# Who issues the first keys, and when the first weight piece comes: the head of a linear attention and token mixer on one core

## The chip, the cores and the metric

The kernel runs on one core of a Trainium2 chip. The metric is the device time of one execution in microseconds, as the median of several executions. A profiled execution gives the trace.

## The reference

Four batches, four heads, 1088 positions, head size 32. First a linear attention with a quadratic feature map, then a mixer over tokens and channels (all float32 or float64 weights):

```python
def phi(x):                       # S1, S2: 8 x 32
    a = einsum('rd,bhsd->bhsr', S1, x)
    b = einsum('rd,bhsd->bhsr', S2, x)
    return einsum('bhsi,bhsj->bhsij', a, b).reshape(..., 64)
q_p, k_p = phi(q), phi(k)
kv = einsum('bhsf,bhsd->bhfd', k_p, v)
z = sum(k_p, axis=2)
x = einsum('bhsf,bhfd->bhsd', q_p, kv) / (einsum('bhsf,bhf->bhs', q_p, z) + 1e-06)
x = x.transpose(0, 2, 1, 3).reshape(4, 1088, 128)
h = maximum(x.T @ w_tok1, 0) @ w_tok2     # per batch: 1088 -> 256 -> 1088
u = x + h.T
out = u + maximum(u @ w_ch1, 0) @ w_ch2   # 128 -> 1536 -> 128
```

The S matrices and the four weights are float64, so they arrive as pairs of 32-bit words.

## The kernel before

**Tiles and stages.** The sequence is cut into nine tiles of 128 positions (`TILES`) and, for queries and the token mixer, into three chunks of 384, 384 and 320 (`CHUNKS`). For each batch the kernel computes the keys' features and `kv` (`keys`, ops `K<b>.*`), the queries' features `qp` (for batch 0 on TensorE, `queries_on_pe`, ops `Q0.*`; for the others through DRAM, `queries_by_dma`), then attention and token mixing (`mixing`, ops `A<b>.*`), and last the channel mixing (`channel_mix`, ops `U<i>.*`), in which each of 12 slices takes a first group of three matmuls (L992, op `.f`), a Relu on ScalarE (L996, `.h`), a difference on VectorE (L999, `.l`) and a second group of three matmuls (L1005, `.s`). A number is carried as a high and a low half, so one product takes three matmuls. The pool `hid` holds the results of four slices.

**Weights.** `wt1`, `wt2`, `wc1` and `wc2` come in pieces named by two digits, weight and piece: `00` to `04`, `10` to `15`, `20` to `22`, `30` to `32`. `convert` turns a piece of 64-bit floats into 32-bit ones: two ScalarE passes over the words (L363 `.abs`, the magnitude of the high word, and L367 `.low`, the rest of the low word), three VectorE steps (L370 `.clamp`, L374 `.shift`, L377 `.merge`) and an addition on GpSimd (L381 or L383, `.add`). `divide_weight` then makes the halves: ScalarE `.hi` (L474) and VectorE or GpSimd `.lo` (L477). S goes the same way, as the op `s`, and everything of batch 0 needs it: `s_c` is the weight of the keys' matmuls, `s_spread` that of the queries'.

**Order.** The order of the instructions of each engine is made when the kernel is built, by a list scheduler (`Plan.run`): each op has costs by engine, a level (the longest cost behind it, plus a boost for its batch, plus an entry of the table `LEAD`), and of the ops that can start first the one with the highest level goes next. `free` and `dma` in it are the starting times that it assumes for the engines and the transfers. Where it expects TensorE to wait, it puts matmuls on the identity (`fill`, L342).

**Loads.** All loads go out on SyncE's queue (SP) in the order of `LOADS`, each ordered behind the one before it (`load`, L346). The load of S is issued ahead of the plan (L322). In `load_k` the keys of batch 0 are two transfers: columns of the first four tiles (`k0a`, 256 KB) and the rest (320 KB); the first lets `K0.p0` (four tiles) start alone, `K0.p4` takes the other five. The queries of batch 0 are one transfer of 544 KB, and all three `Q0.p<g>` wait for it. A piece of 512 columns is 512 KB, v is 594 KB per batch.

Of the kernel before, what the change touches and what calls it, by code (L numbers as in the profile page):

```python
# [9 lines left out]
F32 = mybir.dt.float32  # L10
# [8 lines left out]
P = 128  # L19
B, H, S, D = 4, 4, 1088, 32  # L20
# [10 lines left out]
TILES = tuple((t * P, P) for t in range(NT))  # L31

CUTS = {0: (2, 2, 2, 2, 1), 2: (4, 4, 4), 3: (4, 4, 4)}
LOADS = "k0 q0 00 v0 01 02 03 04 10 11 20 30 q1 12 13 k1 21 31 v1 14 15 22 32".split()


WIDE = 384
# [2 lines left out]
def _spans():  # L40
# [22 lines left out]
KEYS_ON_POOL = set()  # L63

LEAD = {
    "A0.d2": -161700.0,
    "A0.u0": -740800.0,
    "A0.w2": 67900.0,
    "A1.n2": 62000.0,
    "A1.x": 384700.0,  # L70
    "A1.xT3": 472400.0,
    "A2.w0": -38700.0,
    "A2.w1": -1729700.0,
    "A3.w2": -107200.0,
    "K0.kvz": -142200.0,
    "K0.s08": -237500.0,
    "K1.s": -160000.0,
    "K1.v0": 40800.0,
    "K3.c0": 99700.0,
    "K3.p": 103300.0,  # L80
    "K3.s": -300900.0,
    "K3.v4": -498400.0,
    "Q0.a10": 1269000.0,
    "Q0.a20": 461800.0,
    "Q1.m00": -332100.0,
    "Q1.m10": -30800.0,
    "Q1.p": 115700.0,
    "Q3.p": -1683600.0,
    "U0.f": 988300.0,
    "U0.h": 359200.0,  # L90
    "U0.l": -79900.0,
    "U1.f": 653600.0,
    "U11.f": 345700.0,
    "U2.f": 96300.0,
    "U2.l": -115500.0,
    "U2.s": -804700.0,
    "U4.l": 520500.0,
    "U5.s": -35900.0,
    "U6.s": -144500.0,
    "U8.s": -175400.0,  # L100
    "w00.hi": -357200.0,
    "w00.lo": -624600.0,
    "w00.low": 15500.0,
    "w01.add": -162900.0,
    "w01.hi": -266600.0,
    "w01.lo": -1103500.0,
    "w02.hi": -337700.0,
    "w02.lo": -1981200.0,
    "w03.hi": -871700.0,
    "w03.lo": -604900.0,  # L110
    "w03.low": 376600.0,
    "w03.shift": -580100.0,
    "w04.abs": 1406800.0,
    "w04.add": 140400.0,
    "w04.hi": -260600.0,
    "w04.lo": -663100.0,
    "w04.low": 1049700.0,
    "w10.abs": 830500.0,
    "w10.hi": -265000.0,
    "w10.low": 172800.0,  # L120
    "w10.shift": -115500.0,
    "w11.abs": 656200.0,
    "w11.clamp": -128400.0,
    "w11.low": -9800.0,
    "w12.abs": 1523900.0,
    "w12.clamp": -157100.0,
    "w12.hi": -811900.0,
    "w12.lo": -452800.0,
    "w12.low": 1313100.0,
    "w13.abs": 945800.0,  # L130
    "w13.clamp": -534800.0,
    "w13.hi": 621700.0,
    "w13.low": -19300.0,
    "w13.merge": 637100.0,
    "w13.shift": -290300.0,
    "w14.lo": -1439000.0,
    "w14.low": -519800.0,
    "w15.clamp": 19000.0,
    "w15.low": -641500.0,
    "w21.clamp": 156100.0,  # L140
    "w21.low": -51800.0,
    "w22.abs": 140100.0,
    "w30.clamp": 716200.0,
    "w30.low": -55000.0,
    "w31.hi": -429100.0,
    "w32.low": -49100.0,
}


# [35 lines left out]
class Plan:  # L185
# [20 lines left out]
    def run(self, fill):  # L206
        for op in reversed(self.ops):
            cost = op.weight if op.weight is not None else min(op.ways.values()) + LATE.get(min(op.ways, key=op.ways.get), 0)
            op.level = cost + max((n.level for n in op.next), default=0.0)
        for op in self.ops:  # L210
            op.level += op.boost + LEAD.get(op.name, 0.0)
        free = dict.fromkeys(LATE, 0.0)
        free["sp"], free["act"], free["pe"] = 1060.0, 2000.0, 1400.0 + 427 * WARM
        dma, mode = 2800.0, 0

        port = 0.0
        waiting = {op: len(op.before) for op in self.ops}
        ready = [op for op in self.ops if not op.before]

        def clock(s, cost):  # L220
            if s >= WARMED:
                return s + cost
            return s + 2 * cost if s + 2 * cost <= WARMED else WARMED + cost - (WARMED - s) / 2

        while ready:
            best = []
            for op in ready:
                t = max((a.end for a in op.after), default=0.0)
                ok = True
                for k, h in enumerate(op.takes):  # L230
                    q = self.taken.setdefault(h.pool, [])
                    n = self.bufs.get(h.pool, 1) - sum(o.pool == h.pool for o in op.takes[:k])
                    if len(q) >= n:
                        old = q[len(q) - n]
                        if any(u.end is None for u in old.users):
                            ok = False
                            break
                        t = max(t, max((u.end for u in old.users), default=0.0))
                if not ok:
                    continue  # L240
                for e, cost in op.ways.items():
# [24 lines left out]
            if e == "pool" or (e == "dve" and op.port):
                port = f
            if e == "sp":
                dma = max(dma, f + 630.0) + op.bytes / op.rate
                op.end = dma + (1200 if op.bytes > 100000 else 0)  # L270
            else:
                op.end = f + LATE[e]
            op.emit(e)
            ready.remove(op)
            for n in op.next:
                waiting[n] -= 1
                if not waiting[n]:
                    ready.append(n)
        left = [op.name for op in self.ops if op.end is None]
        assert not left, left[:20]  # L280
# [23 lines left out]
def attn_mixer_kernel(ctx: ExitStack, tc: tile.TileContext, qT, kT, v1, s64, wt1, wt2, wc1, wc2, out):  # L304
# [15 lines left out]

    s_raw = const.tile([P, 64], I64, name="s_raw")
    nc.sync.dma_start(s_raw, s64)  # L322
    ident = const.tile([P, P], F32, name="ident")
    make_identity(nc, ident)
    qp = const.tile([P, 2, SP], F32, name="qp")
# [80 lines left out]
        k_hold[b], q_hold[b], v_hold[b] = Hold("k_sb"), Hold("q_sb"), Hold("v_sb")  # L406
    s_loaded = plan.add("s", {"sp": 0.0}, lambda _: None)
    s_loaded.bytes, s_loaded.rate = 65536.0, 395.0
    prev = s_loaded

    def keep(name, b, shape):
        def dst():
# [3 lines left out]

    def load_k(b, after, boost=0.0):
        if not b:

            half = 4 * P  # L420
            first = load("k0a", lambda: keep("k_sb", 0, [P, SP])()[:, :half], kT[0][:, :half], P * half * 4, after, [k_hold[0]], (), boost)
            k_loaded["first"] = first
            return load("k0", lambda: box["k_sb", 0][:, half:], kT[0][:, half:], P * (SP - half) * 4, [first], (), [k_hold[0]], boost)
        return load(f"k{b}", keep("k_sb", b, [P, SP]), kT[b], P * SP * 4, after, [k_hold[b]], (), boost)

    def load_q(b, after, boost=0.0):
        return load(f"q{b}", keep("q_sb", b, [P, S]), qT[b], P * S * 4, after, [q_hold[b]], (), boost)

    def values(b):
        box["v_sb", b] = new("v_sb", [P, 1200])[:, :NT * H * (D + 1)].rearrange("p (t h d) -> p t h d", t=NT, h=H)  # L430
# [2 lines left out]
    def load_v(b, after, boost=0.0):  # L433
        return load(f"v{b}", lambda: values(b), v1[b], P * NT * H * (D + 1) * 4, after, [v_hold[b]], (), boost)

    k_loaded, q_loaded, v_loaded, doubles = {}, {}, {}, {}
    by_kind = {"q": (load_q, q_loaded), "k": (load_k, k_loaded), "v": (load_v, v_loaded)}
    for name in LOADS:
        if name[0] in by_kind:
            get, known = by_kind[name[0]]  # L440
            b = int(name[1])
            prev = known[b] = get(b, [prev])
# [171 lines left out]
    def queries_on_pe(qp_hold):  # L614
# [16 lines left out]
        for g, (c0, cn) in enumerate(CHUNKS):  # L631
# [12 lines left out]
                            rhs=box["q_sb", 0][rows, cs], start=True, stop=True,  # L644
                        )

            projected = plan.add(f"Q0.p{g}", {"pe": 2 * cn * 1.675 + 20}, project, [q_loaded[0]] + spreads, a_holds + b_holds, [q_hold[0]], 0.0, 2)
            for p in range(2):
                a_hold, b_hold, ar_hold, br_hold = a_holds[p], b_holds[p], Hold("ar"), Hold("ar")

# [461 lines left out]
```

## Time and profile before

| | us |
|---|---|
| three timed runs | 222.3, 221.36, 222.7 |
| median | 222.3 |
| the profiled execution | 223.0 |
| its span, first to last instruction | 220.8 |
| TensorE busy (matmul) | 212.9 |
| VectorE busy | 138.6 |
| ScalarE busy | 118.0 |
| GpSimd busy | 80.3 |

The engines are named PE (TensorE matmul), PEld (its weight loads), DVE (VectorE), ACT (ScalarE), POOL (GpSimd) and SPq or ACTq (the DMA issues of SyncE and of ScalarE). A row of the timeline gives the start, the time, the engine, the line, the operation, the tile written and the tiles read, shapes, a count, and in brackets the engine's idle time before it and what ended that. A row of the waits gives who waited for whom: the total, how often, and the longest. The granted clock of TensorE is 0.998 of full speed.

### The profile page before, as it was taken

The page shows a single profiled execution, that of the slowest core. Times are in us where ns is not written, and L with a number is a line of the kernel's source. Part 1 is how long each engine was busy: PE and PEld are TensorE (multiplying, and loading weights), DVE is VectorE, ACT ScalarE, POOL GpSimd, SP SyncE. Part 2 cuts the span into 40 slices and gives each one's busy share as a digit, 9 for nine tenths or more (in the row PEclk, how much of TensorE's full clock was granted, in tenths as well). Part 3 has the DMA queues.
Part 4 walks back from the last instruction along what each step waited for, and adds up shares of the span by engine and source line. Part 5 has one row for each costly group of instructions (what it writes and reads, how often), then busy time and mean ns, then how long its engine had stood idle before and what let it go on. Part 6 is the DMA issues. An engine that isn't in the chain of part 4 may idle for free.

```text
span 220.8 us, 4921 instructions
## 1 busy us (share of the span) xinstructions
PE 212.9 (96%) x1898; PEld 201.6 (91%) x1898; DVE 138.6 (63%) x273; ACT 118.0 (53%) x284; POOL 80.3 (36%) x85
## 2 busy tenths in 40 slices
PE   7898999998999999999999999999999999999994
PEld 7677669888998999999999899999999999999993
DVE  1589999889648466555744355558255645556562
ACT  4497799996436145443443554455235545445551
POOL 2067597997999103840500240544002210000000
PEclk9999999999999999999999999999999999999999
DMA  6999996994103898510060258400610100100000
GB/s 180 368 409 408 403 399 214 198 208 150 37 3 118 246 221 166 146 67 0 3 228 22 63 136 152 180 0 6 210 38 0 39 1 0 36 3 36 0 33 24
DMA packets 11351, 28.42 MB, mean 129 GB/s; under 512 B 1472, under 2 KB 5568, under 8 KB 11328
## 3 DMA queue, kind: packets, MB, share of 16 engines
q1 hardware_dynamic: 11328, 28.11, 41.5%
q8 instruction: 15, 0.25, 0.5%
q14 instruction: 8, 0.07, 0.1%
HBM read 23.27 MB, written 4.83 MB: 127 GB/s over the span
## 4 chain that ended last, share of the span: by engine, by line
PE 79%; ACT 8%; DVE 5%; DMA 4%; issue 2%; SPq 1%; DVEq 0%; ACTq 0%
PE ps_h L992 30%; PE ps_o L1005 30%; PE ps_a L822 4%; PE ps_a L942 4%; DMA doubles<-wt 4%; PE ps_a L760 3%; PE ps_a L551 2%; ACT halves L474 2%; DVE c L370 2%; ACT tail L367 2%; ACT hh L996 2%; PE ps_a L504 2%; PE ps_a L816 1%; ACT c L363 1%; PE ps_a L938 1%
## 5 line engine op out<-in xcount | busy, mean ns | idle before, releaser
L999 DVE SCALAR_TENSOR_TENSOR hl<-ps_h,hh 128x384 fp32r<-128x384 f32 (+2 forms) x144 | 75.5, 534 | 51.3 <-ACT hh L996 47.4
L996 ACT ACTIVATE hh<-ps_h 128x384 fp32r<-128x384 f32 (+2 forms) x144 | 67.6, 474 | 60.4 <-PE ps_h L992 37.3
L992 PE MATMUL ps_h<-uh,halves 128*128 128x384 f32 (+2 forms) x288 | 88.6, 334 | 0.8 <-DVE hl L999 0.7
L1005 PE MATMUL ps_o<-hh,halves 128*128 128x384 f32 (+2 forms) x288 | 70.7, 328 | 0.0
L992 PEld LDWEIGHTS ps_h<-uh,halves 128*128 128x128 f32 x288 | 53.1, 187 | 3.0 <-DVE hl L999 1.6
L1005 PEld LDWEIGHTS ps_o<-hh,halves 128*128 128x128 f32 x288 | 50.7, 188 | 0.5 <-ACT hh L996 0.4
L1005 PE MATMUL ps_o<-hl,halves 128*128 128x384 f32 (+2 forms) x144 | 47.2, 328 | 0.0
L992 PE MATMUL ps_h<-ul,halves 128*128 128x384 f32 (+2 forms) x144 | 47.1, 327 | 0.0
L916 POOL TENSOR_TENSOR ul<-us,uh 128x64 fp32r<-128x64 f32 (+4 forms) x15 | 9.6, 652 | 51.8 <-ACT uh L913 51.7
L1005 PEld LDWEIGHTS ps_o<-hl,halves 128*128 128x128 f32 x144 | 27.0, 188 | 0.3 <-DVE hl L999 0.3
L992 PEld LDWEIGHTS ps_h<-ul,halves 128*128 128x128 f32 x144 | 27.1, 188 | 0.2
L740 POOL TENSOR_TENSOR qp<-qp,br 128x544 f32<-128x544 f32 x12 | 16.2, 1370 | 10.8 <-DMA br<-rows 10.7
L534 DVE TENSOR_TENSOR k_p<-ps_a,a_sb 128x1024 f32<-128x1024 f32 (+1 forms) x12 | 11.0, 953 | 7.1 <-ACT a_sb L514 7.1
L788 POOL TENSOR_TENSOR xl<-x,xh 128x384 fp32r<-128x384 f32 x9 | 9.0, 1020 | 15.2 <-ACT den L768 14.3
L381 POOL TENSOR_TENSOR whole<-c,tail 128x512 int32<-128x512 int32 (+3 forms) x11 | 11.9, 1090 | 4.1 <-DVE c L377 2.6
L367 ACT ACTIVATE tail<-doubles 128x512 int32<-128x512 uint32 (+3 forms) x17 | 10.4, 622 | 2.8 <-DMA doubles<-wt 2.8
L477 POOL TENSOR_TENSOR halves<-whole,halves 128x384 fp32r<-128x384 f32 (+3 forms) x11 | 11.5, 1063 | 0.0
L342 PEld LDWEIGHTS ps_o<-ident 128*128 128x128 f32 x60 | 8.9, 227 | 2.8 <-POOL ident masks.py:199 1.4
L363 ACT ACTIVATE c<-doubles 128x512 f32<-128x512 f32 (+3 forms) x17 | 10.5, 626 | 1.5 <-DMA doubles<-wt 1.1
L342 PE MATMUL ps_o<-ident 128*128 128x128 f32 x60 | 9.7, 318 | 1.4 <-POOL ident masks.py:199 1.4
L377 DVE SCALAR_TENSOR_TENSOR c<-doubles,ps_h 128x512 int32<-128x512 int32 (+3 forms) x17 | 10.3, 611 | 0.1
L374 DVE TENSOR_SCALAR ps_h<-c 128x512 int32<-128x512 int32 (+3 forms) x17 | 10.3, 618 | 0.1
(76 smaller groups left out, 230.2 us busy)
## 6 DMA issues: line engine op xcount, KB each, us to landing
qp<-rows SPq DMA_DIRECT2D x6, 544.0 KB, 9.1
br<-rows SPq DMA_DIRECT2D x12, 272.0 KB
doubles<-wc SPq DMA_DIRECT2D x6, 512.0 KB
v_sb<-v SPq DMA_DIRECT2D x4, 594.0 KB
q_sb<-qT SPq DMA_DIRECT2D x4, 544.0 KB, 12.1
doubles<-wt SPq DMA_DIRECT2D x4, 512.0 KB, 8.6
k_sb<-kT SPq DMA_DIRECT2D x3, 576.0 KB, 6.0
xm<-xb SPq DMA_DIRECT2D x3, 576.0 KB, 2.7
```

Of the source, the lines that this page charges most:

```text
L342: nc.tensor.matmul(spare_ps[:, :P], lhsT=ident, rhs=ident, start=True, stop=True)
L363: nc.scalar.activation(f32(t["c"]), f32(high), AF.Abs)
L367: nc.scalar.activation(t["tail"], low.bitcast(U32), AF.Copy, scale=2.0 ** -29)
L374: nc.vector.tensor_scalar(t["ps"], t["c"], 3, 0x3FFFFFFF, op0=ALU.logical_shift_left, op1=ALU.bitwise_and)
L381: engines[e].tensor_tensor(dst(), t["c"], t["tail"], op=ALU.add)
L477: engines[e].tensor_tensor(halves[w, i][:, 1], f32(whole[w, i] if w < 2 else t["c"]), f32(halves[w, i][:, 0]), op=ALU.subtract)
L534: engines["pool" if on_pool else "dve"].tensor_tensor(t["k_p"][:pn, t0 * H:t1 * H], a.unsqueeze(3).broadcast_to([pn, n, R, R]), t["sb", t0 ...
L740: engines[e].tensor_tensor(qp[:, p, cs], qp[:, p, cs], t["br"][:, p, cs], op=ALU.mult)
L992: nc.tensor.matmul(h_ps[:, :cn], lhsT=part(2, at[2][e][0], l, at[2][e][1] * P, P), rhs=r[:, :cn], start=(m == 0), stop=(m == 2))
L996: nc.scalar.activation(t["hh"][:, :cn], t["h"][:, :cn], AF.Relu)
L999: nc.vector.scalar_tensor_tensor(t["hl"][:, :cn], t["h"][:, :cn], 0.0, f32(t["hh"][:, :cn]), op0=ALU.max, op1=ALU.subtract)
L1005: nc.tensor.matmul(outs[i][:, :cn], lhsT=part(3, at[3][e][0], l, at[3][e][1] * P, P), rhs=r[:, :cn], start=(e == 0 and m == 0), stop=(e == ...
```

## The change

- The first four tiles of batch 0's keys (`k0a`) are issued on ScalarE's queue, ahead of the plan, right after S on SyncE's.
- The queries of batch 0 are loaded in two pieces: the first chunk (384 columns, 192 KB, `q0a`) and the other two (352 KB, `q0b`). `Q0.p0` waits for the first alone, the other two for the second.
- `LOADS` has another order: the weight piece `00` comes between the two pieces of q, ahead of the rest of the keys; `02` and `01` change places, as do `11` and `10`; the values of batch 1 (`v1`), `12` and `q1` come ahead of `20`, and `13` and `k1` ahead of `30`.
- The planner's starting times: SyncE 1100 instead of 1060, ScalarE 2450 instead of 2000, transfers 2350 instead of 2800 (ns).
- The table `LEAD` is another one, with 77 entries instead of 81; all later work can so change its order too.

The arithmetic, and the engine that does each step, are left to the planner as before; no op is added or taken away but the load of q, which is two.

```diff
-LOADS = "k0 q0 00 v0 01 02 03 04 10 11 20 30 q1 12 13 k1 21 31 v1 14 15 22 32".split()
+LOADS = "q0a 00 q0b k0 v0 02 01 03 04 11 10 v1 12 q1 20 13 k1 30 31 21 14 22 15 32".split()
...
 LEAD = {
-    "A0.d2": -161700.0,
-    "A0.u0": -740800.0,
...
+    "A0.d1": -555700.0,
+    "A0.u0": -560600.0,
...
+    "w00.abs": -302800.0,
...
 }
...
-        free["sp"], free["act"], free["pe"] = 1060.0, 2000.0, 1400.0 + 427 * WARM
-        dma, mode = 2800.0, 0
+        free["sp"], free["act"], free["pe"] = 1100.0, 2450.0, 1400.0 + 427 * WARM
+        dma, mode = 2350.0, 0
...
     nc.sync.dma_start(s_raw, s64)
+    k_first = pool.tile([P, SP], F32, name="k_sb", bufs=1)
+    nc.scalar.dma_start(k_first[:, :4 * P], kT[0][:, :4 * P])
...
-    prev = s_loaded
+    first_keys = plan.add("k0a", {"sp": 0.0}, lambda _: None, (), [k_hold[0]], (), order=[s_loaded])
+    first_keys.bytes, first_keys.rate = P * 4 * P * 4, 395.0
+    box["k_sb", 0] = k_first
+    prev = first_keys
...
         if not b:
-
-            half = 4 * P
-            first = load("k0a", lambda: keep("k_sb", 0, [P, SP])()[:, :half], kT[0][:, :half], P * half * 4, after, [k_hold[0]], (), boost)
-            k_loaded["first"] = first
-            return load("k0", lambda: box["k_sb", 0][:, half:], kT[0][:, half:], P * (SP - half) * 4, [first], (), [k_hold[0]], boost)
+            return load("k0", lambda: k_first[:, 4 * P:], kT[0][:, 4 * P:], P * (SP - 4 * P) * 4, after, (), [k_hold[0]], boost)
...
+    def load_q_part(name, after):
+        if name == "q0a":
+            box["q_sb", 0] = new("q_sb", [P, S])
+        c0, c1 = (0, CHUNKS[0][1]) if name == "q0a" else (CHUNKS[0][1], S)
+        return load(name, lambda: box["q_sb", 0][:, c0:c1], qT[0][:, c0:c1], P * (c1 - c0) * 4, after, [q_hold[0]] if name == "q0a" else (), () if name == "q0a" else [q_hold[0]], 0.0)
...
-    k_loaded, q_loaded, v_loaded, doubles = {}, {}, {}, {}
+    k_loaded, q_loaded, v_loaded, doubles = {"first": first_keys}, {}, {}, {}
     by_kind = {"q": (load_q, q_loaded), "k": (load_k, k_loaded), "v": (load_v, v_loaded)}
     for name in LOADS:
-        if name[0] in by_kind:
+        if name[:2] == "q0":
+            prev = q_loaded[name] = load_q_part(name, [prev])
+            q_loaded[0] = prev
+        elif name[0] in by_kind:
...
-            projected = plan.add(f"Q0.p{g}", {"pe": 2 * cn * 1.675 + 20}, project, [q_loaded[0]] + spreads, a_holds + b_holds, [q_hold[0]], 0.0, 2)
+            projected = plan.add(f"Q0.p{g}", {"pe": 2 * cn * 1.675 + 20}, project, [q_loaded["q0b" if g else "q0a"]] + spreads, a_holds + b_holds, [q_hold[0]], 0.0, 2)
```

More of the change, by code (lines that the diff above doesn't have):

```diff
@@ L86 @@
[L86 to L144, printed above, removed]
@@ L145 @@
-    "w31.hi": -429100.0,
-    "w32.low": -49100.0,
+    "A0.d1": -555700.0,
+    "A0.u0": -560600.0,
+    "A0.uh11": 104200.0,
+    "A1.n1": -49400.0,
+    "A1.t0": -2740300.0,
+    "A1.t2": -151100.0,
+    "A1.w1": 62300.0,
+    "A1.w2": 8600.0,
+    "A1.xT2": -39400.0,
+    "A2.n1": -1700.0,
+    "A3.hT": 283900.0,
+    "A3.t0": -83800.0,
+    "A3.t2": 200600.0,
+    "A3.x": -3000.0,
+    "K1.c0": 794400.0,
+    "K1.kvz": -219200.0,
+    "K1.s": -466900.0,
+    "K1.v4": -624700.0,
+    "K2.v4": -87400.0,
@@ new lines @@
+    "K3.p": 106500.0,
+    "K3.s": -424600.0,
+    "Q0.a10": 329100.0,
+    "Q0.a11": 15300.0,
+    "Q0.b01": 106100.0,
+    "Q0.b11": 118600.0,
+    "Q0.b21": -463100.0,
+    "Q0.p2": -41000.0,
+    "Q1.m00": -343100.0,
+    "Q1.p": 984200.0,
+    "Q1.r00": -208500.0,
+    "Q2.p": -407800.0,
+    "Q3.p": -4550800.0,
+    "U0.h": 292700.0,
+    "U0.l": -244900.0,
+    "U0.s": -166900.0,
+    "U1.l": -384100.0,
+    "U1.s": -1745700.0,
+    "U11.s": -142600.0,
+    "U2.f": -1323400.0,
+    "U3.s": -219400.0,
@@ new lines @@
+    "U4.s": 961300.0,
+    "U7.f": 36100.0,
+    "U7.s": 108600.0,
+    "v3": 57500.0,
+    "w00.abs": -302800.0,
+    "w00.lo": -1280000.0,
+    "w01.abs": 441700.0,
+    "w01.lo": -702700.0,
+    "w01.low": -2394000.0,
+    "w02.abs": 664700.0,
+    "w02.hi": -2462400.0,
+    "w02.lo": -1309900.0,
+    "w02.low": 229900.0,
+    "w03.lo": -1228200.0,
+    "w04.clamp": 166400.0,
+    "w04.lo": -4428900.0,
+    "w10.abs": 54000.0,
+    "w10.clamp": 33900.0,
+    "w10.hi": 56400.0,
+    "w10.shift": -1254400.0,
@@ L147 @@
+    "w11.abs": 23200.0,
+    "w11.hi": 1621300.0,
+    "w11.low": -2690200.0,
+    "w11.shift": 320300.0,
+    "w12.lo": -1170700.0,
+    "w12.low": 472000.0,
+    "w13.hi": -2129100.0,
+    "w13.low": -3429400.0,
+    "w13.shift": -272800.0,
+    "w14.abs": 572700.0,
+    "w14.add": -517600.0,
+    "w20.abs": -119500.0,
+    "w21.abs": 1097300.0,
+    "w22.clamp": 4200.0,
+    "w22.low": 94600.0,
+    "w30.hi": 363500.0,
+    "w30.shift": -486800.0,
 }
```

18 lines of the change are left out of this document (removed).

## The prediction

> **What bounds the kernel now.** I read the page's totals first, then the busy time in stretches of the span, then the waits of each engine, and last the order of events in the first 40 us.
>
> ```profile
> span 220.8 us, 4921 instructions
> PE 212.9 (96%) x1898; PEld 201.6 (91%) x1898; DVE 138.6 (63%) x273; ACT 118.0 (53%) x284; POOL 80.3 (36%) x85
> ```
>
> Over the whole span TensorE (PE) is full and VectorE (DVE) looks free. The average hides two stages, which the windows separate (columns: busy us of PE, PEld, DVE, ACT, POOL with their instructions, clock, DMA share, GB/s):
>
> ```profile
> 0.00:10.00 10.00, 7.67 (x70) 6.58 (x71) 3.56 (x7) 3.98 (x12) 1.16 (x9) 1.00 0.77 259
> 10.00:20.00 10.00, 9.80 (x158) 7.91 (x159) 8.44 (x16) 9.52 (x24) 5.58 (x5) 1.00 1.03 409
> 20.00:30.00 10.00, 8.92 (x118) 6.95 (x115) 9.69 (x24) 7.20 (x19) 6.58 (x7) 1.00 1.03 404
> 30.00:40.00 10.00, 9.68 (x112) 8.28 (x111) 9.97 (x19) 9.77 (x23) 8.88 (x8) 1.00 0.80 269
> ```
>
> From 10 to 40 us DVE is busy for 8.44, 9.69 and 9.97 of each 10 us: it turns the weights' 64-bit words into floats, piece by piece. PE's own busy time up to 33 us is partly the filler matmuls on the identity (L342), so it is no load. PE's real load begins with the first channel matmul, and from there it hardly pauses:
>
> ```profile
> 33.14 0.63 PE L992 MATMUL ps_h<-uh,halves 128*128 128x384 f32 x1
> 16.07 2.50 PE L342 MATMUL ps_o<-ident 128*128 128x128 f32 x20
> PEld ps_h L992 <- DVE hl L999: 1.4, 2, 1.0
> ```
>
> So the end is set by when the front hands over to that row at 33.14 us, plus some 187 us of packed PE work that the change leaves as it is. The question is how much earlier DVE gets through its work in front of 33.14. It has few holes there; these are all that its waits between 5 and 34 us show:
>
> ```profile
> DVE c L370 <- ACT c L363: 2.0, 1, 2.0
> DVE k_p L534 <- ACT a_sb L514: 1.9, 1, 1.9
> DVE qp L670 <- ACT xT L660: 0.9, 1, 0.9
> ```
>
> The 1.9 ends when batch 0's first key products can begin. The 2.0 and the 0.9 can be seen in DVE's own sequence:
>
> ```profile
> 5.94 2.69 DVE L534 TENSOR_TENSOR k_p<-ps_a,a_sb 128x1024 f32<-128x1024 f32 x3 [1.86 <-ACT a_sb L514]
> 10.62 0.43 DVE L370 TENSOR_SCALAR c<-c 128x512 f32<-128x512 f32 x1 [2.00 <-ACT c L363]
> 10.99 0.55 DVE L670 TENSOR_TENSOR qp<-xT,ps_h 128x384 f32<-128x384 f32 x1
> 11.46 0.69 DVE L374 TENSOR_SCALAR ps_h<-c 128x512 int32<-128x512 int32 x1
> 12.18 0.69 DVE L377 SCALAR_TENSOR_TENSOR c<-doubles,ps_h 128x512 int32<-128x512 int32 x1
> 13.73 0.49 DVE L670 TENSOR_TENSOR qp<-xT,ps_h 128x320 f32<-128x320 f32 x1 [0.86 <-ACT xT L660]
> ```
>
> All key products are done at 8.63, because both parts of the keys came first; then DVE has nothing until the first weight piece (00) has landed and ScalarE (ACT) has taken its magnitude. After 14.2 us it never waits again before 33. **2.86 us of holes, then a full engine: that is what the change can win.**
>
> **The change, part by part.** First the landings. A wait of ACT or PE that a DMA ends gives a true landing time:
>
> ```profile
> 9.37 0.66 ACT L367 ACTIVATE tail<-doubles 128x512 int32<-128x512 uint32 x1 [2.79 <-DMA doubles<-wt]
> 9.94 0.66 ACT L363 ACTIVATE c<-doubles 128x512 f32<-128x512 f32 x1
> 8.24 0.92 PE L642 MATMUL ps_a<-q_sb,s_spread 64*128 64x384 f32 x4 [0.98 <-DMA q_sb<-qT]
> 12.14 0.68 ACT L363 ACTIVATE c<-doubles 128x512 f32<-128x512 f32 x1 [0.42 <-DMA doubles<-wt]
> ```
>
> q landed by 8.24, piece 00 by 9.37, piece 01 by 12.14. From q to 01 there are 512 + 594 + 512 = 1618 KB in 3.90 us, or 415 KB a us; I use this rate.
>
> *Piece 00 ahead.* In front of it stood s 64, keys 576 and q 544 KB; now s 64, the keys' first part 256 and q's first part 192. That is 672 KB less, 1.6 us at 415 KB a us. Early transfers are slower (below), so it may be up to 2.1 us at 315.
>
> *Keys issued by ACT.* SP issues one transfer after another:
>
> ```profile
> 0.74 0.39 SPq L322 DMA_DIRECT2D s_raw<-s  x1
> 1.19 0.88 SPq L346 DMA_DIRECT2D k_sb<-kT  x2
> 2.11 0.43 SPq L346 DMA_DIRECT2D q_sb<-qT  x1
> 1.50:2.00 0.50, 0.50 (x3) 0.50 (x4) 0.00 (x0) 0.50 (x1) 0.26 (x2) 1.00 0.27 79
> 2.00:2.50 0.50, 0.50 (x4) 0.50 (x4) 0.00 (x0) 0.01 (x1) 0.00 (x0) 1.00 0.80 142
> 2.50:3.00 0.50, 0.50 (x4) 0.50 (x3) 0.00 (x0) 0.29 (x2) 0.00 (x0) 1.00 0.61 168
> 3.00:3.50 0.50, 0.50 (x5) 0.50 (x4) 0.43 (x3) 0.12 (x1) 0.00 (x0) 1.00 1.14 325
> 4.00:4.50 0.50, 0.50 (x4) 0.50 (x3) 0.08 (x1) 0.38 (x2) 0.00 (x0) 1.00 1.13 315
> ```
>
> In these 0.5 us windows the DMA share is 0.80 and 0.61 at 142 and 168 GB/s until 3.0 us, and full only from 3.0 on, at 315 to 325. With the keys in another queue, each later transfer of SP is issued one step, 0.44 us, sooner, and that time is not hidden, as the engines were not full. I count 0.4 us on every landing; bounds 0 and 0.87 (the 0.275 MB missing against 315 GB/s in 1.5 to 3.0 us). Otherwise SP's order of issue moves past nothing but other loads. Splitting q adds one issue of 0.43 us on SP, behind queued bytes: q's first part, 00 and the rest of q hold 1056 KB, 2.5 us of transfer for 1.3 us of issue, so it costs nothing.
>
> The Trainium skill speaks against this part: the page "DMA: Bandwidth & Descriptors", section "Issuing engines are not separate DMA queues", says that issuing from several engines saves only the sequencer's time to initiate, usually small beside the transfer. By that the 0.4 would be near 0 and the gain below about 1.2; the shares 0.80 and 0.61 say that here the sequencer's time was not hidden.
>
> *What it costs ACT.* The issue goes ahead of the table load, which sits under a wait:
>
> ```profile
> 0.73 1.28 ACT L363 ACT_TABLE_LOAD   x1 [0.73 <-PEq L1104]
> 2.71 0.26 ACT L363 ACTIVATE s_c<-s_raw 128x64 f32<-128x64 f32 x1 [0.70 <-DMA s_raw<-s]
> ```
>
> ACT waits 0.70 for s; 0.43 of issue fits in it and the table is ready at about 2.45. If s were to land as before, the price is nothing. But s (64 KB) now shares the engines with 256 KB issued at the same moment. Its delay is not shown by this trace: it is bounded by 0 (s goes through first) and 0.8 us (s ends with the keys, 262 KB at 315 GB/s). All of the front hangs on s, so I take 0.3, nearer to 0 because SP's 64 KB are the smaller load.
>
> *DVE's new sequence*, with these landings and DVE's start kept at 5.94. The first key product takes 1.23 (the same 1024-wide product alone, quoted below), to 7.17. The q chunk whose load landed early (64 + 256 + 192 KB, at about 5.5) gives a multiply of 0.55, to 7.72. Piece 00 lands at 9.37 - 1.6 - 0.4 = 7.4 at the latest of my terms and 6.9 at the other bound; I take 7.0, and its two ACT passes (0.66 each, 1.25 together) end at 8.3: a hole of 0.58. Clamp, shift and merge (0.43 + 0.69 + 0.69) end at 10.1. The keys' second part has 1696 KB with all before it, as piece 00 had, so it lands at 9.37 - 0.4 = 9.0; its 20 of 36 matmuls and their copy (0.71 and 0.27) are done at 10.0, and the other two products (2.69 - 1.23 = 1.46) end at 11.6. Two more q multiplies (0.49 and 0.55) end at 12.6. The next weight piece lands at 12.14 - 0.4 = 11.7 and, with its two ACT passes (1.3), is ready at 13.0: a hole of 0.4. Then pieces come every 512/415 = 1.23 us and cost DVE 1.81, so it stays full.
>
> ```profile
> 4.91 1.27 PE L504 MATMUL ps_a<-s_c,k_sb 128*64 128x64 f32 x36
> 5.64 0.27 ACT L514 COPY a_sb<-ps_a 128x128 f32<-128x128 f32 x1 [0.47 <-PE ps_a L504]
> 30.48 1.23 DVE L534 TENSOR_TENSOR k_p<-ps_a,a_sb 128x1024 f32<-128x1024 f32 x1
> ```
>
> Holes before 2.86, after 0.58 + 0.4 = 1.0: **gain 1.9; less 0.3 for s: 1.6 us**. Everything behind (DVE full to 40 us, then PE) should move by that. It displaces no PE work: PE fills 2.50 us with the identity at 16.07, so there is room for what has to be done sooner.
>
> *Other weights later.* Behind 11 and 10 now come v1, 12 and q1, and then 20; 13 and k1 before 30. At 415 KB a us piece 20 lands at about 21.6 (18.3 before) and 30 at about 25.1 (19.5 before). The cover is that both were converted long after landing:
>
> ```profile
> 29.91 1.33 POOL L383 TENSOR_TENSOR c<-c,tail 128x512 int32<-128x512 int32 x1 [0.42 <-DVE c L377]
> 31.41 0.62 ACT L474 CAST halves<-c 128x512 fp32r<-128x512 f32 x1
> 32.16 1.29 POOL L477 TENSOR_TENSOR halves<-c,halves 128x512 fp32r<-128x512 f32 x1
> 36.83 1.30 POOL L477 TENSOR_TENSOR halves<-c,halves 128x512 fp32r<-128x512 f32 x1 [1.07 <-ACT halves L474]
> 38.13 0.36 PEld L1005 LDWEIGHTS ps_o<-hh,halves 128*128 128x128 f32 x2
> ```
>
> The POOL rows of L477 are the two pieces' last steps, and the first output matmul loads at the very moment (38.13) when the second ends. The conversion needs some 5.7 us of work (0.66, 0.43, 0.69, 0.69, 1.33, 0.62, 1.29), so 25.1 leaves slack if the ranks give it its turn. I price it at nothing; without that cover it is the last rival.
>
> *Ranks.* They change only the order of ready work. The waits above (1.4 us of PEld behind DVE's hl) are what a better order past 33 us could still give; a worse one can cost as much. I take 0 and keep plus and minus 1.4 for the range.
>
> *Sum.* The profiled execution took 223.0 for its span of 220.8; less 1.6 it is 221.4 (span 219.2). The median of the three is 222.3, 0.7 below that execution, so the forecast is **220.7**. About 1% (2.2 us) is what a measurement of this kernel can tell from no change.
>
> **The rivals.**
>
> *Both holes close and the order gets better.* Piece 00 lands at 6.9, magnitude first, nothing left of the 2.86: the gain is 2.9, so 219.4, and with a part of the ranks' 1.4 us it is below 219. For it: DMA has no other limit before 13 us. Against: two ACT passes stand between landing and DVE. Chance 0.20.
>
> *s is late.* The keys' 256 KB travel beside s and it lands 0.8 later, with nothing of it absorbed: 1.9 - 0.8 = 1.1, so 221.2. For it: s is the smallest load and now goes out together with a bigger one; against: it is also the first of its queue. Chance 0.14. The Trainium skill, page "DMA: Bandwidth & Descriptors", section "Queues, rings and completion order", says that each DMA engine takes turns between queues packet by packet, which would end s together with most of the keys; no row here shows two queues at once.
>
> *The gain is lost again at ACT.* ACT is busy 9.77 of the 10 us from 30 to 40, so DVE's earlier pieces queue there for their hi halves: no change, 222.3. Against: ACT has 2.79 us of hole before 9.37 as well, and 7.20 of 10 from 20 to 30. Chance 0.16. It would be the same time if the change does not do what it says, that is if piece 00 does not land before about 9.
>
> *Slower: piece 30 decides.* It took 38.13 - 19.5 = 18.6 us from landing to split. If it takes even 15.5 after 25.1, it is ready at 40.6, while the output matmuls, 1.6 sooner, want it at 36.5. Channel matmuls cannot run ahead, as four hidden buffers hold their results, so PE stands for up to 4.1 us and 2.5 are lost net: 224.8. It decides from a split later than 38.1. For it: DVE and ACT are at their fullest there. Against: the rest between landing and split was waiting by rank, not work. Chance 0.10.
>
> **How the numbers follow.** Forecast 220.7 (219.7 to 221.6 by the terms' bounds): 0.40; the rivals 0.20, 0.14, 0.16 and 0.10. The range 218.8 to 223.0 takes in the first three rivals with some of the ranks' 1.4 us, and leaves out the slower one and the outer tails, together under 0.2. Faster by over 1% is below 220.1: most of the first rival and the low edge of the forecast, 0.25. Slower by over 1% is above 224.5: half of the last rival, 0.06. Within 1%: 0.69.
>
> **What would show it.** Right: ACT takes 00 up at about 7 instead of 9.37; DVE's wait of 2.0 shrinks under 0.7; it is idle about 1 us from its first product to 14; the first channel matmul (L992) begins at 31.5 instead of 33.14; piece 30's split ends before 36.5. Wrong: s is taken up past 3.0; 00 past 8; a PE wait for POOL's halves near 37; or an earlier L992 with new PE waits behind DVE's hl, which would show that the new ranks gave the gain back after the handover.

## The result, and the profile after

The changed kernel takes **223.91 us** (median of six runs, 223.58 to 224.65), the kernel before 221.83 in the runs beside it (220.71 to 222.7). The ratio is 1.0101, with a 95% interval of 1.0072 to 1.0131 (ratios, here and below, are estimated from the single runs, so they differ a little from the quotient of two medians, 1.0094 here): **2.1 us slower**, where 220.7 was forecast and 223.0 was the upper end of the range. The profiled execution took 223.74 for a span of 222.0. The profiled execution of the kernel before stood 1.2 above its median (223.0 against 221.83), so the two spans differ by 1.2 only.

First the totals of the changed kernel, and its busy time in stretches (columns as before):

```profile
span 222.0 us, 4865 instructions
PE 213.5 (96%) x1878; PEld 200.4 (90%) x1878; DVE 141.1 (64%) x273; ACT 117.9 (53%) x284; POOL 80.1 (36%) x85
...
0.00:10.00 10.00, 7.90 (x41) 5.82 (x42) 3.24 (x8) 5.13 (x13) 1.17 (x9) 1.00 0.78 269
10.00:20.00 10.00, 9.91 (x178) 7.71 (x179) 9.09 (x17) 8.25 (x23) 5.35 (x5) 1.00 0.95 338
...
50.00:60.00 10.00, 8.57 (x47) 8.12 (x47) 9.21 (x18) 4.35 (x9) 7.11 (x7) 1.00 0.22 76
```

VectorE (DVE) is busy 2.5 us longer than before (141.1 against 138.6) with the same 273 instructions. It did not get more work: some of its instructions got longer. TensorE (PE) has a hole from 50 to 60 us, where it should be packed: busy 8.57 of 10 us, against 9.69 before.

The head, in order of time (start, time, engine, line, operation, and in brackets the idle time before it and what ended that):

```profile
0.73 0.41 ACTq L320 DMA_DIRECT2D k_sb<-kT  x1
1.36 2.93 PE L340 MATMUL ps_o<-ident 128*128 128x128 f32 x12 [1.36 <-POOL ident masks.py:199]
3.60 0.26 ACT L361 ACTIVATE s_c<-s_raw 128x64 f32<-128x64 f32 x1 [1.15 <-DMA s_raw<-s]
5.03 1.12 PE L510 MATMUL ps_a<-s_c,k_sb 128*64 128x64 f32 x16 [0.73 <-DVE s_c L381]
6.08 1.65 PE L648 MATMUL ps_a<-q_sb,s_spread 64*128 64x384 f32 x4
7.35 0.66 ACT L365 ACTIVATE tail<-doubles 128x512 int32<-128x512 uint32 x1 [0.89 <-DMA doubles<-wt]
```

Piece 00 is taken up at 7.35 (9.37 before), as hoped. But s is taken up at 3.60 (2.71 before). The new plan also puts only 12 filler matmuls at the head, which end at 4.29; before there were 16, to 4.98. So PE pauses for 0.73 before the keys, and the matmuls behind the pause run at half pace: the four query matmuls take 1.65 where the same four took 0.92 before. DVE's sequence from there:

```profile
6.50 1.23 DVE L540 TENSOR_TENSOR k_p<-ps_a,a_sb 128x1024 f32<-128x1024 f32 x1 [1.52 <-ACT a_sb L520]
8.60 0.43 DVE L368 TENSOR_SCALAR c<-c 128x512 f32<-128x512 f32 x1 [0.88 <-ACT c L361]
9.98 0.56 DVE L676 TENSOR_TENSOR qp<-xT,ps_h 128x384 f32<-128x384 f32 x1 [0.22 <-ACT xT L666]
11.87 1.56 DVE L540 TENSOR_TENSOR k_p<-ps_a,a_sb 128x1024 f32<-128x1024 f32 x2 [0.74 <-ACT a_sb L520]
```

It starts 0.56 later (6.50 against 5.94) and has 0.88 + 0.22 + 0.74 = 1.84 us of holes, against 2.86. So at 14 us the change stands 0.46 us ahead by this count. It is lost by the handover to TensorE's channel work, and there is a second loss after it. DVE, GpSimd (POOL) and PE around 47 us:

```profile
33.89 0.63 PE L998 MATMUL ps_h<-uh,halves 128*128 128x384 f32 x1
...
46.37 2.29 POOL L483 TENSOR_TENSOR halves<-whole,halves 128x384 fp32r<-128x384 f32 x2
48.61 1.50 POOL L483 TENSOR_TENSOR halves<-c,halves 128x512 fp32r<-128x512 f32 x1
...
47.52 2.78 DVE L368 TENSOR_SCALAR c<-c 128x512 f32<-128x512 f32 x2
50.22 0.55 DVE L1005 SCALAR_TENSOR_TENSOR hl<-ps_h,hh 128x384 fp32r<-128x384 f32 x1
...
50.82 0.44 PE L1011 MATMUL ps_o<-hl,halves 128*128 128x384 f32 x1 [0.69 <-DVE hl L1005]
52.00 0.45 PE L998 MATMUL ps_h<-uh,halves 128*128 128x384 f32 x1 [0.74 <-DVE hl L1005]
```

Two clamps (L368, of 512 columns for piece 32 and of 320 for piece 14; the row shows the first one's shape) take 2.78 together; the runs below have them at 0.66 and apart at 0.32 for the smaller. They end where GpSimd's operations end: the second at 50.3, just after GpSimd's row of 48.61 (1.50, to 50.1). The difference `hl` stands behind them, and PE waits for it twice, 1.43 us in all. Before, the same pair stood at the same place:

```profile
46.94 1.47 POOL L740 TENSOR_TENSOR qp<-qp,br 128x544 f32<-128x544 f32 x1
46.77 1.83 DVE L370 TENSOR_SCALAR c<-c 128x512 f32<-128x512 f32 x2
48.52 0.54 DVE L999 SCALAR_TENSOR_TENSOR hl<-ps_h,hh 128x384 fp32r<-128x384 f32 x1
```

The pair took 1.83 there, behind one GpSimd operation instead of two. These rows were in the trace that the prediction was made from.

### The profile page after: what moved, and what is told of

Read it like the earlier page. It is cut to its first block, busy times and chain, and to the rows that moved or that the text cites. A ratio compares the mean times of both kernels' runs of the same rounds, so it can differ in the third digit from the quotient of the medians.

```text
span 222.0 us, 4865 instructions
## 1 busy us (share of the span) xinstructions
PE 213.5 (96%) x1878; PEld 200.4 (90%) x1878; DVE 141.1 (64%) x273; ACT 117.9 (53%) x284; POOL 80.1 (36%) x85
## 4 chain that ended last, share of the span: by engine, by line
PE 78%; DVE 10%; ACT 6%; issue 3%; DMA 1%; POOL 1%; DVEq 0%; POOLq 0%
PE ps_o L1011 30%; PE ps_h L998 30%; PE ps_a L828 4%; PE ps_a L948 4%; PE ps_a L766 3%; DVE c L368 3%; DVE ps_h L372 2%; ACT halves L480 2%; PE ps_a L557 2%; PE ps_a L510 2%; DVE c L375 2%; ACT hh L1002 1%; DMA s_raw<-s 1%; ACT tail L365 1%; DVE hl L1005 1%
## 5 line engine op out<-in xcount | busy, mean ns | idle before, releaser
L922 POOL TENSOR_TENSOR ul<-us,uh 128x64 fp32r<-128x64 f32 (+4 forms) x15 | 9.7, 657 | 50.1 <-ACT uh L919 50.0
L794 POOL TENSOR_TENSOR xl<-x,xh 128x384 fp32r<-128x384 f32 x9 | 9.0, 1015 | 15.2 <-ACT den L774 14.2
L368 DVE TENSOR_SCALAR c<-c 128x512 f32<-128x512 f32 (+3 forms) x17 | 11.6, 704 | 0.9 <-ACT c L361 0.9
L372 DVE TENSOR_SCALAR ps_h<-c 128x512 int32<-128x512 int32 (+3 forms) x17 | 10.4, 617 | 0.2
L766 PEld LDWEIGHTS ps_a<-kvz,qp 128*64 128x64 f32 x288 | 9.0, 137 | 1.7 <-issue 0.9
L375 DVE SCALAR_TENSOR_TENSOR c<-doubles,ps_h 128x512 int32<-128x512 int32 (+3 forms) x17 | 10.4, 609 | 0.1
```

The lines of the kernel that those rows point to most:

```text
L368: nc.vector.tensor_scalar(f32(t["c"]), f32(t["c"]), LEAST, MOST, op0=ALU.max, op1=ALU.min)
L372: nc.vector.tensor_scalar(t["ps"], t["c"], 3, 0x3FFFFFFF, op0=ALU.logical_shift_left, op1=ALU.bitwise_and)
L375: nc.vector.scalar_tensor_tensor(t["c"], high, -(1 << 30), t["ps"], op0=ALU.bitwise_and, op1=ALU.bitwise_or)
L766: nc.tensor.matmul(x_ps[c:c + 64, o:o + 2 * (D + 1)], lhsT=qp[:, p, s0 + c:s0 + c + 64], rhs=kvz_all[b % 2][:, p, :2 * (D + 1)], start=Tru ...
```

## The experiments

Four theories of the loss, by the letters that the expectations use. **A**: s lands late, and TensorE is slow at the head. **B**: DVE's new order puts the divisions of batch 0's attention behind weight steps. **C**: the values of batch 1 (v1), now ahead of piece 20, stop SyncE's queue. **D**: DVE's clamps stand behind GpSimd's operations. For most kernels the changed kernel's order of instructions was written out and one entry or a few moved in it, so all else stays as it was. In the short diffs `move(a, b)` puts entry a right behind entry b. Times of before beside the runs were 221.47 to 221.69.

**Keys issued by SyncE again.**

```diff
-    nc.scalar.dma_start(k_first[:, :4 * P], kT[0][:, :4 * P])
+    nc.sync.dma_start(k_first[:, :4 * P], kT[0][:, :4 * P])
```

> The changed kernel, with the first keys issued by SyncE behind S instead of by ScalarE; the order of every engine's other work is the changed kernel's. Theory A (S lands late because the keys travel beside it, and TensorE runs out of fillers before S is ready, so its matmuls go at half pace until about 10.6 us): ScalarE takes S up at 2.7 instead of 3.60, the first 16 keys' matmuls take 0.6 us instead of 1.12, the first products start at 5.9 instead of 6.50, and the time falls by 0.5 to 1.5 us from 223.9. Theory B (the new order of VectorE, with batch 0's divisions behind weight steps, loses the time whatever S does): S is early too, but the first channel matmul stays at 33.5 to 34 us and the time within 0.4 of 223.9. Theory C (the load of v1 stops SyncE's queue until 15.2 us): no change, 223.9.

Measured: 223.13, ratio 1.0065 (1.0038 to 1.0093). The head of this kernel:

```profile
2.55 0.26 ACT L361 ACTIVATE s_c<-s_raw 128x64 f32<-128x64 f32 x1 [0.54 <-DMA s_raw<-s]
4.58 1.12 PE L510 MATMUL ps_a<-s_c,k_sb 128*64 128x64 f32 x16 [0.29 <-DMA k_sb<-kT]
5.63 1.65 PE L648 MATMUL ps_a<-q_sb,s_spread 64*128 64x384 f32 x4
```

s is back at 2.55, so the keys beside it are what delays it by 1.05 us. But PE now waits 0.29 for the keys, and stays at half pace all the same. The interval touches that of the changed kernel: s late by itself is not shown to be the loss.

**Two more filler products** (four matmuls in the trace, 16 at the head as before), so that PE does not pause before the keys.

```diff
-    fill(WARM)
+    fill(WARM + 2)
```

> The changed kernel with two more filler products at the start (16 matmuls in the trace instead of 12), everything else in its order. If the pause of TensorE from 4.29 to 5.03 us is what keeps its matmuls slow until 10.6 (part of theory A), the 4 query matmuls take 0.9 us instead of 1.65, VectorE's first product starts at 6.2 to 6.4 instead of 6.50, the keys' second part is projected before 10.0 instead of at 10.63, and the time falls by 0.3 to 0.8 us from 223.9. If the slow pace does not come from the pause, or nobody waits for TensorE there, 223.9 plus or minus 0.3.

Measured: 222.54, ratio 1.0036 (1.0011 to 1.0061), 1.4 us less than the changed kernel, with intervals that do not meet. The matmuls at the head, and the handover:

```profile
4.89 0.69 PE L510 MATMUL ps_a<-s_c,k_sb 128*64 128x64 f32 x16
5.51 0.92 PE L648 MATMUL ps_a<-q_sb,s_spread 64*128 64x384 f32 x4
...
33.51 0.63 PE L998 MATMUL ps_h<-uh,halves 128*128 128x384 f32 x1
```

No pause, and full pace: 0.92 again. The keys' second part is projected at 9.00 instead of 10.63. The waits for `hl` behind the handover are unchanged, 0.7 twice. That the fillers are worth about 1.4 us is measured; how the gain reaches the end is not shown by this trace. DVE's clamp of the second piece comes 1.29 earlier (12.51 instead of 13.80), but the handover only 0.38. In between PE waits 1.7 for ScalarE's `xT`, and the granted clock is 0.81 from 15 to 20 us and 0.85 from 20 to 25. This profiled execution took 223.66, the slowest of its twelve. So this half of theory A is supported by the times, and its path stays open.

**Divisions first.**

```diff
+        move("A0.d1", "A0.n1")
+        move("A0.d2", "A0.n2")
```

> The changed kernel with two operations of VectorE moved: batch 0's divisions of the second and third group go right behind the ScalarE step that each needs, ahead of a clamp, a merge and shifts of the weights. Theory B: the division of the second group ends near 21.5 instead of 24.72, TensorE's second part of the token matmul starts at about 23 instead of 25.39, the first channel matmul comes at 32.5 to 33 instead of 33.89, and the time falls by 0.7 to 1.4 us from 223.9. Theories A and C: the front is late for another reason, the weights moved behind become late instead, and the time stays within 0.4 of 223.9.

Measured: 223.9, ratio 1.0095 (1.0064 to 1.0126). The two divisions came at 21.01 and 22.96 instead of 23.11 and 24.16, and then PE waited for another engine:

```profile
PE ps_a L883 <- ACT h L861: 1.3, 1, 1.3
```

The handover stayed at 33.83. Theory B falls: the divisions were late, but ScalarE was not ready for what follows them.

**v1 behind k1.** In the changed kernel SyncE issues nothing between 8.56 and 15.22:

```profile
5.89 2.66 SPq L344 DMA_DIRECT2D doubles<-wt  x3
15.22 0.33 SPq L344 DMA_DIRECT2D v_sb<-v  x1
```

v1 needs a buffer that batch 0's last values matmul frees at 15.2, and every later piece stands behind it.

```diff
+        move("v1", "k1")
```

> The changed kernel with the load of batch 1's values issued behind batch 1's keys, so that it no longer waits for its buffer at the head of SyncE's queue. Theory C: SyncE has no gap of issue from 8.6 to 15.2 us, the 16th and 17th us carry 400 GB/s instead of 200, and the time falls by 0.3 to 1 us from 223.9. Theories A and B: the transfers close up, but nothing waited for them, 223.9 plus or minus 0.3.

Measured: 223.2, ratio 1.0074 (1.0045 to 1.0102). The transfers are full again (408 GB/s from 10 to 20 us, 338 in the changed kernel), the handover is not earlier (34.14). Alone it may be worth 0.7 us or nothing.

**The issue by ScalarE alone**, put into the kernel before.

```diff
-            nc.sync.dma_start(dst(), src)
+            (nc.scalar if name == "k0a" else nc.sync).dma_start(dst(), src)
```

> The kernel before, with only the issue of the first keys moved to ScalarE's queue; loads, their other order, ranks and the order of all engines are those of before (16 filler matmuls at the head). S late by 0.9 us (theory A): ScalarE takes S up at 3.5 instead of 2.71, VectorE's first product starts at 6.3 to 6.6 instead of 5.94, TensorE's fillers end at about 5.0 as before so that its matmuls stay fast, and the 0.4 us of earlier landings are worth less than that: 222.0 to 222.5 against 221.7 before. If the earlier landings decide (the prediction's reading): 221.3. If neither reaches the end: 221.7 plus or minus 0.2.

Measured: 221.77, ratio 1.0004 (0.9978 to 1.003): no gain to be seen, though the interval still takes in the 0.4 us that the prediction gave it. In its trace s is late as in the changed kernel (3.50), while the first weight piece is taken up 0.53 sooner than before (9.37), and the handover comes at 32.78 (33.14). The keys' matmuls run at half pace for a while without any pause ahead of them (2.19 us for 36, against 1.27 before):

```profile
5.08 2.19 PE L504 MATMUL ps_a<-s_c,k_sb 128*64 128x64 f32 x36
8.84 0.67 ACT L367 ACTIVATE tail<-doubles 128x512 int32<-128x512 uint32 x1 [1.18 <-DMA doubles<-wt]
```

The trace has a use of its own, since its order is that of the kernel before in a typical execution (221.44). The clamp pair in it, and GpSimd at that moment:

```profile
46.44 0.66 DVE L370 TENSOR_SCALAR c<-c 128x512 f32<-128x512 f32 x2
47.20 0.56 DVE L999 SCALAR_TENSOR_TENSOR hl<-ps_h,hh 128x384 fp32r<-128x384 f32 x1
...
45.27 1.31 POOL L383 TENSOR_TENSOR c<-c,tail 128x512 int32<-128x512 int32 x1
47.76 1.37 POOL L740 TENSOR_TENSOR qp<-qp,br 128x544 f32<-128x544 f32 x1 [1.19 <-DMA br<-rows]
```

GpSimd happened to wait for a transfer, and the pair took 0.66. In the profiled execution of before the same operation of GpSimd had started at 46.94, and the pair took 1.83. So this meeting varies from execution to execution.

**The old table of ranks in the changed kernel.**

```diff
-    "A0.d1": -555700.0,
...
+    "A0.d2": -161700.0,
...
```

> The changed kernel's loads and first keys, with the table of ranks of the kernel before. Theory D (the clamps of VectorE stand behind GpSimd's operations for 3.2 us more in the changed kernel, 11.7 against 8.5 us in all, because of the order that the new ranks made): the clamps fall back to about 9 us, and the time to 221 to 222.5. Theory A (S late and TensorE slow at the head): the head is the same, 223 to 224. The order was made by the old ranks for other landings, so it can also be worse than both, above 224.5; then it says nothing of either.

Measured: 245.82, ratio 1.1057 (1.1007 to 1.1106). The ranks belong to their load order and can't be tried alone; the run tells nothing of the theories.

**The clamps apart.** The clamp of piece 14 goes behind the merge of piece 32, three DVE steps later.

```diff
+        move("w14.clamp", "w32.merge")
```

> The changed kernel with one VectorE operation moved: of the two clamps that follow each other at 47.5 us and hold VectorE for 2.78 us behind GpSimd, the second goes behind the merge of the first. Theory D: the Relu differences between them come about 1 us sooner, TensorE's two waits of 0.7 us at 50 to 52 us fall to at most one, and the time falls by 0.5 to 1.2 us from 223.9. If the clamp waits for GpSimd just as long in its new place, or TensorE has other work missing there, 223.9 plus or minus 0.3.

Measured: **221.85, ratio 1.0000** (0.9971 to 1.0029). One entry moved takes back 2.06 us of 2.08 by the medians and all of the loss by the ratios, and the interval lies clear of the changed kernel's. DVE, and all that PE then waits for after the handover:

```profile
47.38 1.42 DVE L388 TENSOR_SCALAR c<-c 128x512 f32<-128x512 f32 x1
48.72 0.54 DVE L1025 SCALAR_TENSOR_TENSOR hl<-ps_h,hh 128x384 fp32r<-128x384 f32 x1
...
50.96 0.32 DVE L388 TENSOR_SCALAR c<-c 128x320 f32<-128x320 f32 x1
...
PE ps_h L1018 <- DVE hl L1025: 0.3, 1, 0.3
```

`hl` comes at 48.72 instead of 50.22, and 0.3 of the 1.4 us of waits is left. The handover of this profiled execution (34.08) is no earlier, so the trace accounts for 1.1 us; the rest of the 2.06 is within the two intervals and is not traced.

**GpSimd's operations away from the pair**, with DVE's order left alone.

```diff
+        move("w13.lo", "w32.add")
+        move("w01.lo", "w13.lo")
```

> The changed kernel with VectorE's order left as it is, clamp pair and all; only GpSimd's order is another: its two low halves of pieces 13 and 01 (the row 46.37 2.29 x2) come after the addition of piece 32, so that beside the clamp pair at 47.5 stands one operation (the low half of 22) and not two. Theory D (a clamp cannot run beside a GpSimd operation): the pair shrinks from 2.78 to between 0.9 and 1.8 us, the difference behind it (hl) comes 1 to 2 us earlier than 50.22, TensorE's waits for it (0.69 and 0.74) shrink, and the kernel takes 222.0 to 223.0 (0.9 to 1.9 less). Rival (the pair is on the path of hl by its place in VectorE's order, whatever GpSimd does, or the loss lies in other ops that the ranks moved): hl comes at most 0.4 earlier and the time stays at 223.6 or above.

Measured: 223.46, ratio 1.0103 (1.0066 to 1.014): no gain in time, though the mechanism did what theory D said:

```profile
47.62 0.66 DVE L389 TENSOR_SCALAR c<-c 128x512 f32<-128x512 f32 x2
48.20 0.55 DVE L1026 SCALAR_TENSOR_TENSOR hl<-ps_h,hh 128x384 fp32r<-128x384 f32 x1
...
48.56 1.30 POOL L504 TENSOR_TENSOR halves<-c,halves 128x512 fp32r<-128x512 f32 x1 [2.04 <-ACT halves L501]
...
56.82 0.44 PE L1032 MATMUL ps_o<-hh,halves 128*128 128x384 f32 x1 [0.87 <-POOL halves L504]
```

The pair now falls into a gap of GpSimd (2.04 idle before 48.56) and shrinks from 2.78 to 0.66 in the same DVE order, so it was GpSimd that held it. But the two operations, done later, now stand in front of the halves of piece 32, which end at 56.8 (55.0 in clamp_apart), and PE waits 0.87 for those instead. My expectation of 222.0 to 223.0 missed that.

**The same clamp moved in the kernel before.**

```diff
+        move("w14.clamp", "w32.merge")
```

> The kernel before with the one edit that helped the changed one: the clamp of piece 14 moved behind the merge of piece 32. Its pair took 1.83 there, and hl after it came at 48.52. If the pair costs by its length (theory D), the kernel gains what the pair loses beyond one clamp, at most 0.9 us: 220.8 to 221.7. If before had slack at that place (TensorE's longest wait for hl is 1.0 in all), it stays at 221.4 to 222.0. If the edit is a gain of its own that has nothing to do with the change, it is faster by about 2 us (219.7), and then clamp_apart says nothing of the change's loss.

Measured: 221.91, ratio 1.0009 (0.9984 to 1.0035), no gain. So the move is no improvement by itself; it undoes something that the change brought.

**Three mends together.**

```diff
+        move("w14.clamp", "w32.merge")
+        move("v1", "k1")
-    fill(WARM)
+    fill(WARM + 2)
```

> The changed kernel with two more filler products at the head, the load of v1 behind k1, and the second clamp apart, together. If the losses add up (1.4 and 0.7 us measured for the first two, 0.5 to 1.2 us expected of the third): 220.7 to 221.4, level with the kernel before or just under it. If they are one and the same loss (VectorE full until 40 us, whoever is late in front): about 222.4, as the fillers alone.

Measured: 221.02, ratio 0.9975 (0.9949 to 1.0), first channel matmul at 31.92. It is the fastest kernel of the study, 0.6 us below the one before at the very edge of what its interval can tell.

**The three mends without v1's move.**

```diff
-        move("v1", "k1")
```

> three_mends (221.02, first channel matmul at 31.92) with batch 1's values back at their place in the changed kernel's load order: the clamp of piece 14 apart and two more filler matmuls are what is left. Theory C (v1 at the head of SyncE's queue waits for its buffer, and all later pieces with it, and that costs time): the first channel matmul comes at 32.6 or later and the kernel takes 221.6 to 222.2. Rival (VectorE has enough pieces in hand through the 6 us in which SyncE stands, so the values' place is worth nothing): the handover stays at 31.8 to 32.3 and the time at 220.8 to 221.4.

Measured: 221.56, ratio 0.9989 (0.9965 to 1.0013), between what the two theories expected. The granted clock fell to 0.72 from 20 to 25 us in its profiled execution, so its handover (34.39) can't be compared. The two medians differ by less than their intervals: theory C stays open.

**And the front's clamps too.** In three_mends two clamps took 1.73 at 15.61, beside an addition on GpSimd.

```diff
+        move("w03.clamp", "Q0.m20")
+        move("w04.clamp", "w03.clamp")
```

> three_mends (221.02) with the clamps of pieces 03 and 04 moved behind piece 01's merge and the third queries' multiply, out of the addition on GpSimd that made them take 1.73 at 15.61. Theory D: they take at most 1.3 there, VectorE comes through the front 0.3 to 0.8 us sooner, the first channel matmul begins at 31.1 to 31.6 instead of 31.92, and the kernel takes 220.2 to 220.8. Rival (GpSimd's next operations make other steps wait, or ScalarE is what holds the front by now): the handover stays within 0.2 of 31.92 and the time at 221.0.

Measured: 221.06, ratio 0.9979 (0.9947 to 1.001). The rival was right:

```profile
17.18 0.49 DVE L699 TENSOR_TENSOR qp<-xT,ps_h 128x320 f32<-128x320 f32 x1 [1.00 <-ACT xT L689]
17.58 0.62 DVE L391 TENSOR_SCALAR c<-c 128x512 f32<-128x512 f32 x2
```

The pair takes 0.62, and 1.00 us of waiting for ScalarE has come in its place. The first channel matmul begins at 31.82 (31.92). A long clamp in the front costs nothing as long as the next step waits for something else anyway.

**All together.** The span splits at the first channel matmul; what comes after it is packed PE work, and PE's own waits in it are listed by the chain of waits:

| kernel | first channel matmul | rest of the span | PE's waits in the rest | median of runs |
|---|---|---|---|---|
| act_issue_alone (order of before) | 32.78 | 186.6 | 0 | 221.77 |
| before | 33.14 | 187.7 | 0.7 | 221.83 |
| before_clamp_apart | 33.37 | 186.8 | 0.2 | 221.91 |
| changed | 33.89 | 188.1 | 1.4 | 223.91 |
| clamp_apart | 34.08 | 186.8 | 0.3 | 221.85 |
| pool_gap | 33.97 | 187.7 | 1.1 | 223.46 |
| three_mends | 31.92 | 186.9 | 0.3 | 221.02 |
| four_mends | 31.82 | 186.8 | 0.3 | 221.06 |

The rest is 186.6 plus PE's waits, within 0.4 us, in every row. The loss thus has two parts: a handover that is 0.75 later than in before's profiled execution and 1.11 later than in act_issue_alone's, and 0.4 to 1.5 more behind it, by the same two. The measured 2.1 lies between the sums, 1.2 and 2.6. The second part is shown by experiment. For the first, more fillers and v1's move together brought the handover from 34.08 (clamp_apart) to 31.92 (three_mends) in one trace each, so these two can mend it. How the fillers, the clamps in the front and v1 share it is not shown: the fillers' gain of 1.4 us by the medians is more than the whole first part, their own trace has the handover only 0.38 earlier, and the fillers together with the clamp moved gave less (221.56) than the two gains added would (2.06 and 1.37 off 223.91).

## Why the prediction was wrong, step by step

- **Piece 00 at about 7.0, DVE full from 14 us on.** Right: taken up at 7.35, and no hole after 13.4 us up to the handover.
- **The keys' issue by ScalarE gives 0.4 on every landing.** Right for the landings, not seen in the time. In act_issue_alone the pieces 00 and 01 are taken up at 8.84 and 11.60 instead of 9.37 and 12.14; in the changed kernel 00 is taken up at 7.35, against 8.34 in keys_on_sync. But alone the issue gave no measurable gain (1.0004, with 0.4 us still inside the interval). The sentence of the Trainium skill, page "DMA: Bandwidth & Descriptors", section "Issuing engines are not separate DMA queues", that spoke against the term has the sequencer's time alone saved, and about one issue is what the landings gained; that it is small agrees with the time.
- **s late by 0.3.** Mis-sized: 0.89 (3.60 against 2.71). The rival had 0.8 for it, the upper bound, and the case came out there. The sentence from the Trainium skill on queues that take turns packet by packet, page "DMA: Bandwidth & Descriptors", section "Queues, rings and completion order", agrees with the row.
- **TensorE at the head.** Missed. Nothing in the working asks what PE does while it waits for s. With four filler matmuls less it paused 0.73 us and then ran at half pace until past 10 us, so the keys' second part was projected at 10.63, where I had it done at 10.0. The two more filler products were worth 1.4 us; how much of that is the pace is not shown.
- **Holes of 1.0 left.** 1.84, and DVE's start, which I kept at 5.94, came 0.56 later. Together 0.46 us ahead instead of the 1.6 in the sum.
- **A clamp takes 0.43.** This is the step that failed most. I took one row for all and never looked at how the same instruction varies. In before the row did stand for its own shape; the long clamps were of smaller ones (line, shape, count, total us, mean ns, and the idle time before them):

```profile
L370 DVE TENSOR_SCALAR c<-c 128x512 f32<-128x512 f32 x10 | 4.2, 434 | 2.0 <-ACT c L363 2.0
L370 DVE TENSOR_SCALAR c<-c 128x320 f32<-128x320 f32 x2 | 1.8, 902 | 0.0
L370 DVE TENSOR_SCALAR c<-c 128x256 f32<-128x256 f32 x1 | 1.4, 1370 | 0.0
```

  In the changed kernel the ten of 512 columns take 658 ns on average, the two of 320 take 1302, and the one of 256 takes 281. DVE's time in the clamps, before and after, from 4 to 33 and from 33 to 60 us (columns: DVE busy, clock, DMA share, GB/s):

```profile
4.00:33.00 29.00, 5.06 (x11) 1.00 1.02 393
33.00:60.00 27.00, 3.44 (x6) 1.00 0.64 166
```

```profile
4.00:33.00 29.00, 6.30 (x12) 1.00 0.98 366
33.00:60.00 27.00, 5.43 (x6) 1.00 0.59 184
```

  The first fence is before, the second the changed kernel: 1.2 us more in the front (0.1 of it is the end of S's own clamp, the twelfth), enough to turn the 0.46 ahead into about the 0.75 behind, and 2.0 more after it.
- **Ranks at 0, plus or minus 1.4.** The bound was about right and the value wrong: the two waits for `hl`, 1.43 us, are what the new order brought. I had named this sign ("new PE waits behind DVE's hl") but expected it with an earlier handover. Since the ranks could not be tried alone, whether they or the shift of everything by some tenths made the pair meet two operations of GpSimd is open; the GpSimd order next to it is another one (two low halves where before had one query multiply).
- **Other weights later, at no price.** Not refuted: no PE wait for halves near 37. But I missed that v1, moved ahead, waits for a buffer and holds SyncE for 6.7 us; its cost lies between nothing and 0.7 us.
- **The gain is lost again at ScalarE (0.16).** It was not what happened, but divisions_first and four_mends show that ScalarE is the next limit in the front.
- **The chances.** Slower by over 1% had 0.06, all of it on piece 30. The measured 1.0101 is on that bound, by a mechanism that no rival had.

## What to carry to other kernels

Before pricing an instruction from one row, list all rows of its line, in every shape, and see what runs beside the long ones: an engine whose busy time grows with the same number of instructions is being held by another. When a load is moved earlier, ask what the engines do while they wait for the load that it now travels beside, and when one is put at the head of a queue, ask which buffer it waits for. And where the front hands over to a packed stage, look at the first engine that the packed stage will wait for, not at the front alone.

## What the runs showed of the hardware

*A short pause of TensorE goes with a long stretch at half pace.* The four query matmuls took 0.92 us at full pace (before, two more fillers). They took 1.65 in all seven traces with a pause ahead of the keys' matmuls: 0.29 us in keys_on_sync, and 0.51 to 0.79 in the changed kernel, divisions_first, v1_behind_k1, old_ranks, clamp_apart and pool_gap. Without a recorded pause the pace can be half for a while too, but full pace came by about 7 us: in act_issue_alone the 36 matmuls of the keys took 2.19 instead of 1.27, and in three_mends the keys' 16 took 1.12 and the four of the queries 1.34. The profile's granted clock showed 1.00 from 0 to 10 us in all of these. The Trainium skill, page "TensorE: Matmul & The Clock Gate", Part 1, has a free-running window of about 3.4 us that TensorE must fill before it gets its full clock. That fits: a pause that falls into such a window would cost a whole further one. No run here shows where a window begins, so this is a reading and not shown.

*Clamps and GpSimd exclude each other; the other DVE steps kept their times.* A clamp of 512 columns took 0.43 alone and 1.42 beside a GpSimd operation; single rows of `hl` with 384 columns, which read PSUM, took 0.52 to 0.56 in all traces. From before to the changed kernel the mean of the 512-column clamps went from 434 to 658 ns, while the shift (L374, L372) stayed at 689 and the merge (L377, L375) at 682 and 678. The Trainium skill, page "SBUF — State Buffer", section "SBUF: two separate sides", says that VectorE's two-port operations and GpSimd lock one pair of ports for a whole instruction. The rows agree, and add the price: the same two clamps took from 0.66 to 2.78 us.
